# Routed attention and a feed-forward block: the second pair's rows loaded at the start, the first queries on two queues, a second PSUM bank in the last block

## The chip, the cores and the metric

The kernel runs on one core of a Trainium2 chip. The metric is the device time of one execution in microseconds (us); less is better. A core has five engines with an instruction queue each: TensorE (PE; its weight loads are shown apart as PEld), VectorE (DVE), ScalarE (ACT), GpSimd (POOL) and SyncE (SP). They wait for one another by semaphores only. Loads and stores are DMA transfers: an engine's queue issues them, here mostly SP's (queue q1 in the profile) and some ACT's (q10), and 16 DMA engines move the data.

## The reference

Routed attention over 4 batches, 8 heads, 768 tokens and head dimension 64, and then a feed-forward block over the 3072 tokens:

```python
q_assign = argmax(einsum('bhsd,hcd->bhsc', q_n, c_n))      # 16 centroids per head
k_assign = argmax(einsum('bhsd,hcd->bhsc', k_n, c_n))
mask = q_assign[:, :, :, None] == k_assign[:, :, None, :]
scores = where(mask, scale * matmul(q, k.T), -1e9)
attn = softmax(scores)
x = matmul(attn, v)                                        # -> (3072, 512)
h = x @ w_in                                               # 512 -> 2048
g = h * clip(h + 3.0, 0.0, 6.0) / 6.0
out = g @ w_out                                            # 2048 -> 512
```

A query sees only the keys whose nearest centroid is its own. All is in float32; the weights come as 64-bit floats and are decoded in the kernel.

## The kernel before, in words

Heads are worked on in pairs, two heads side by side on the 128 partitions, 16 pairs in all. The first half of the pairs (g below `FIRST` = 8) is computed with full score tiles and a mask that is added on PE; the second half is computed later from rows sorted by cluster. The feed-forward block is interleaved as filling work, and ends the kernel alone.

*What a full pair needs.* `load` (L187 to L202) brings queries and keys, 192 KB per head, into one tile `qk`, and the values into `vt`. All are issued on SP. The tile `qk` has one buffer (`qkp`), so the next pair's rows can be loaded only when this pair's are turned. `turn` (L309) turns 12 blocks of 128 x 128 on PE in three parts of four blocks. Each part goes into a PSUM tile `pqk` of the rotating pool `psum_m` (two banks), and a copy on ACT (of pair 0's third part on DVE) brings it to `xf`. `cluster_scores` multiplies with the centroids (PE tile `pcs`, L337, copied by ACT to `cs`), `route` turns that back (`pr`), takes the maximum on DVE (`mx`) and makes the `one_hot` tile; `route_turn` turns it (`po`, L379) and copies it, scaled, to `xm`, the mask operand: the first part on ACT, pair 0's second part on DVE.

*The loop.* One step treats two blocks of keys (n and n + 1, 12 blocks per pair). `scores` (L400) adds the mask product of `xm` and the product of `xf` in a PSUM tile `ps` of which there are two; `exponentials` (L423, ACT) makes `ex` from it; `key_sums` adds them up on POOL; `attn_v` (L443, PE) multiplies those of the step before with `vt` into `pv`, the single bank of `psum_v`. Between these stand, at fixed places of the order, the preparation of the next pair (`prep_items`: `turn` parts 0 and 1 in step r = 0, part 2 in r = 2, cluster scores in r = 4, and so on) and the decoding of weight chunks (`raw`, 512 KB each, three buffers; `split` runs a total on ACT, L228, and the first step on DVE, L232, into a PSUM tile of the single bank of `psum_t`). The order on every engine is the order of the Python code: nothing is rescheduled.

*The start.* The centroids are loaded on ACT's queue; queries, keys, values and a weight chunk on SP's. `idle` (L288) issues transposes of the identity whose results nobody uses: 18 before pair 0's rows, 5 between its parts, ahead of the centroids' transpose `pc` (L302), and 5 behind. Then come the cluster scores of pair 0, the unmasked part of its first scores (`scores_qk`), the routing, and the loop.

*The end.* A feed-forward block multiplies 256 tokens by a scheme with seven products (`down`, parts 0 to 6) whose results are the halves of two PSUM tiles `X` and `Y`; DVE adds (L705) and stores (`keep`, L709) give four output pieces of 128 KB. Parts 2 and 5 write the first half of `Y`, parts 3 and 6 the second. After part 6 DVE adds for two output pieces; the last is stored from ACT's queue in the last block. After it all engines branch on a flag (L1691) over a general path that is not taken.

Of the kernel before, what the change touches and what calls it, by code (L numbers as in the profile page):

```python
# [8 lines left out]
F32 = mybir.dt.float32  # L9
# [7 lines left out]
B, H, S, D = 4, 8, 768, 64  # L17
# [102 lines left out]
def fast_path(ctx, tc, ok, q, k, v, centroids, moe_w_in, moe_w_out, out):  # L120
# [60 lines left out]
    def scratch(shape, name, dtype=F32):  # L181

        if st["early"]:
            return psum_m.tile(shape, dtype, name=name, tag="m")
        return psum_t.tile(shape, dtype, name=name, tag="t")
# [3 lines left out]
    def load(g, *names):  # L189
        if g > FIRST or (g == FIRST and "v" in names):  # L190
            return
        b, h = divmod(2 * g, H)
        for name in names:
            if name == "v":
                dst = st["v", g] = vp.tile([P, 2, NCH, D], F32, name="vt")
            elif name == "q":
                st["qk", g] = qkp.tile([P, 2, NCH, 2, D], F32, name="qk")
            if name != "v":
                dst = st["qk", g][:, "qk".index(name)]
            src = {"q": q, "k": k, "v": v}[name]  # L200
            for t in range(2):
                nc.sync.dma_start((dst[:, t] if name == "v" else dst[:, :, t]), src[b, h + t].rearrange("(p j) d -> p j d", p=P))  # L202

# [64 lines left out]
    def constants():  # L270
        make_identity(nc, ident)
        for t in range(2):
            nc.vector.tensor_reduce(
                out=parity[:, t : t + 1],
                in_=ident.rearrange("p (h t c) -> p t h c", t=2, c=C)[:, t], axis=AX.XY, op=ALU.max,
            )
        nc.gpsimd.memset(half_c, 0.5)
        nc.gpsimd.memset(low_c, 1.0 / BOUND)
        nc.gpsimd.memset(ones, 1.0)
        nc.gpsimd.memset(w_low, W_LOW)  # L280
        nc.gpsimd.memset(one_hot, 0.0)

        idle(18)

    def idle(count):
        warm = psum_t.tile([P, 4, P], F32, name="warm", tag="t")
        for i in range(count):
            nc.tensor.transpose(out=warm[:, i % 4], in_=ident, identity=ident)  # L288
# [17 lines left out]

    def turn(g, part):  # L309
        if part == 0:  # L310
            st["xf", g] = xp.tile([P, NC2, P], F32, name="xf")
        qk, xf = st["qk", g], st["xf", g]
        pt = scratch([P, 4, P], "pqk")
        for i in range(4):
            j = part * 4 + i
            if g == 0 and j == NCH:

                idle(5)
                centroid_turn()
            nc.tensor.transpose(out=pt[:, i], in_=qk[:, j // NCH, j % NCH], identity=ident)  # L320
        dst = xf[:, part * 4 : part * 4 + 4]

        if g == 0 and part == 2:
            nc.vector.tensor_copy(out=dst, in_=pt)
        else:
            nc.scalar.copy(out=dst, in_=pt)
        if part == 2:
            st.pop(("qk", g))
# [63 lines left out]
    def scores_qk(n):  # L392
        st["ps", n] = psum_s.tile([P, 2, 512], F32, name="ps")
        scores_part(n, st["xf", where(n)[0]], True, False)
# [191 lines left out]
    def ffn_items(b):  # L586
# [109 lines left out]
        def product(bank, half, kind, w, first, last, again, chunks=range(HF)):  # L696
            for i in chunks:
                nc.tensor.matmul(  # L698
                    bank[:, half * HC : (half + 1) * HC], lhsT=g_sb[:, kind, i], rhs=w[:, i],
                    start=(first and i == 0), stop=(last and i == HF - 1),  # L700
                    skip_group_check=again,
                )

        def add(out_, in0, in1):
            nc.vector.tensor_tensor(out=out_, in0=in0, in1=in1, op=ALU.add)  # L705

        def down(m, part):
            def keep(chunk, half, y, queue=nc.sync):
                queue.dma_start(out_v[b, 2 * m + chunk][:, half * HC : (half + 1) * HC], y)  # L709

            def multiply(second):
                if part < 2:
                    h = range(part * HF // 2, (part + 1) * HF // 2)
                    if second:
                        product(st["X"], 1, 5, st["T2"], False, True, False, h)
                    else:
                        product(st["X"], 0, 0, wb[0][0], True, False, False, h)
                    return
                kind, bank, half, w = (
                    (4, "Y", 0, st["T1"]), (1, "Y", 1, st["T3"]),  # L720
                    (2, "X", 0, wb[1][0]), (6, "Y", 0, wb[1][1]), (3, "Y", 1, st["T4"]),
                )[part - 2]
                h = range(second * HF // 2, (second + 1) * HF // 2)
                product(st[bank], half, kind, w, part == 2, part in (3, 4, 6), part > 3, h)

            def begin():
                raise_gates()
                if part == 0:
                    pool_x = st["psum_y"] if (b, m) == (0, 0) else psum_m
                    st["X"] = pool_x.tile([P, DM], F32, name="X", tag="m")  # L730
                    st["y0"] = yp.tile([P, DM], F32, name="y0", tag="y0")
                elif part == 2:
                    pool_y = psum_m if (b, m) == (0, 0) else st["psum_y"]
                    st["Y"] = pool_y.tile([P, DM], F32, name="Y", tag="m")
                    st["y1"] = yp.tile([P, DM], F32, name="y1", tag="y1")
                multiply(0)

            def end():
                multiply(1)
                if part == 0:  # L740
                    finish()
                if (b, m, part) == (B - 1, NHC - 1, 6):
                    st["good"] = nc.values_load(ok[0:1, 0:1], min_val=0, max_val=1)
                if part == 4:
                    token_sums(*divmod(b * NHC + m + 1, NHC))
                y0, y1 = st["y0"], st.get("y1")
                if part == 1:
                    nc.scalar.copy(out=y0[:, HC:], in_=st["X"][:, HC:])
                    add(y0[:, HC:], y0[:, HC:], st["X"][:, 0:HC])
                elif part == 3:  # L750
                    add(y1[:, 0:HC], y0[:, HC:], st["Y"][:, HC:])
                    add(y1[:, HC:], y1[:, 0:HC], st["Y"][:, 0:HC])
                    keep(1, 1, y1[:, HC:])
                elif part == 4:
                    nc.scalar.copy(out=y0[:, 0:HC], in_=st["X"][:, 0:HC])
                    keep(0, 0, y0[:, 0:HC])
                elif part == 6:
                    add(y1[:, 0:HC], y0[:, HC:], st["Y"][:, HC:])
                    keep(1, 0, y1[:, 0:HC])
                    add(y0[:, HC:], y0[:, HC:], st["Y"][:, 0:HC])  # L760

                    keep(0, 1, y0[:, HC:], nc.scalar if st["last"] else nc.sync)
                if (b, m) == (0, 0):
                    for i in ([HF - 1, HF - 2], [5], [4], [], [3, 2], [0], [1])[part]:
                        make_first_sums(i)
                    if part in (0, 1):
                        weight_sums(6 + part)
                    elif part in (2, 3):
                        weight_sums(2 + part)

            return [begin, end]
# [461 lines left out]
    def prep_items(g, r):  # L1233

        if g > FIRST:
            return []
        turns = [lambda part=part: turn(g, part) for part in range(3)]
        if g == FIRST:
            return {
                0: turns[:2], 2: turns[2:], 4: [lambda: cluster_scores(g)], 6: [lambda: own_clusters(g)],  # L1240
            }.get(r, [])
        one_hots = [lambda: route_turn(g, 0), lambda: route_turn(g, 1)]
        return {
            0: turns[:2], 2: turns[2:], 4: [lambda: cluster_scores(g)], 6: [lambda: route(g)],
            8: one_hots[:1], 10: one_hots[1:],
        }.get(r, [])
# [39 lines left out]
    with tc.manual_schedule():  # L1286
        nc.scalar.dma_start(cen, centroids.rearrange("h c d -> (h c) d"))
        load(0, "q", "k")
        constants()
        load(0, "v")  # L1290
        load_weights(0)
        centroid_norm()
        for part in range(3):
            turn(0, part)
        idle(5)
        nc.vector.tensor_copy(out=ident_q, in_=ident)
        load(1, "q", "k")
        load_weights(1)
        cluster_scores(0)
        scores_qk(0)  # L1300
        route(0)
        scores_qk(1)
        for part in range(2):
            route_turn(0, part)

        for n in range(0, total + lag_d + 2, 2):
            g, r = divmod(n, per_pair)
# [418 lines left out]
```

## Time and profile before

| | |
|---|---|
| median of 3 runs | 949.89 us (947.76 to 950.37) |
| profiled execution | 947.94 us, its span 946.1 us |
| PE busy | 928.3 us, 98% of the span |
| DVE, ACT, POOL busy | 591.6, 349.5, 583.9 us |
| moved by DMA | 124.23 MB |

The span runs from the first to the last instruction of the profiled execution; the time has 1.84 us more around it. A row of the timeline has the start in us, the duration in us (of several like instructions together where "x" and a count stand at its end), engine, line, operation, output tile and inputs, and in brackets how long the engine had been idle before it and what released it. "SPq" and "ACTq" are queues that issue DMAs. A row of a table of stretches has the stretch, its length, and the busy time of each engine within it with the number of instructions.

### The profile page before, as it was taken

Reading aid. Unit: us, or ns where it says so; the run is one execution under the profiler, and the core shown is the slowest. Engines: PE = TensorE matmul, PEld = TensorE weight load, DVE = VectorE, ACT = ScalarE, POOL = GpSimd, SP = SyncE. Lnnn points to the kernel's source line nnn. Section 1 sums busy time; section 2 is a strip of 40 time slices with the busy share of each in tenths; the row PEclk is TensorE's granted clock in tenths of the full one; section 3 lists DMA queues with packets and bytes.
Section 4 is the critical chain, followed back from the end, with each engine's and each line's share of the span. In section 5 each row is a group of like instructions: output and inputs, shape, how many; then the busy total and the mean of one; then the engine's idle time right before and its main releaser. Section 6 shows DMA issues by size and latency. Waiting matters only on the chain.

```text
span 946.1 us, 17635 instructions
## 1 busy us (share of the span) xinstructions
PE 928.3 (98%) x6358; PEld 726.5 (77%) x6358; DVE 591.6 (63%) x1294; ACT 349.5 (37%) x731; POOL 583.9 (62%) x1314
## 2 busy tenths in 40 slices
PE   8999999989999999999999999999999999999997
PEld 5444444555798798797887988978888799999996
DVE  6789889899976375284483474564571554536261
ACT  5888877766112232233232132241331311212020
POOL 3878777769366677787777777777777060303030
PEclk9999999999999999999999999999999999999999
DMA  7345555361364648482683654754753233323120
GB/s 192 108 134 157 134 156 165 109 174 46 96 209 141 153 137 175 130 220 78 171 201 100 166 158 128 192 151 113 176 161 99 77 99 113 106 69 110 56 68 26
DMA packets 174351, 124.23 MB, mean 131 GB/s; under 512 B 134064, under 2 KB 152496, under 8 KB 174256
## 3 DMA queue, kind: packets, MB, share of 16 engines
q1 hardware_dynamic: 151936, 76.04, 31.2%
q10 hardware_dynamic: 13104, 34.38, 12.7%
q0 software_dynamic: 9216, 12.60, 4.4%
q8 instruction: 52, 0.85, 0.4%
q14 instruction: 43, 0.35, 0.1%
HBM read 94.67 MB, written 28.31 MB: 130 GB/s over the span
## 4 chain that ended last, share of the span: by engine, by line
PE 70%; DVE 2%; DMA 1%; ACT 0%; POOL 0%; issue 0%; SPq 0%; ACTq 0%
PE Y L698 18%; PE uY L659 15%; PE X L698 13%; PE uX L659 12%; PE pv L1116 3%; PE ps L1077 3%; PE ps L919 2%; PE pv L1077 1%; PE pd L1140 1%; PE pcs L337 1%; PE ps L1157 1%; DMA piece<-kvd 1%; DVE g_sb L649 0%; DVE g_sb L502 0%; DVE g_sb L670 0%; DVE sx L670 0%
## 5 line engine op out<-in xcount | busy, mean ns | idle before, releaser
L433 POOL TENSOR_TENSOR acc<-acc,ex 128x768 f32<-128x768 f32 x64 | 123.8, 1935 | 26.0 <-ACT ex L423 22.4
L1034 POOL DMA_INDIRECT qd<-qn,pos x96 | 96.3, 1003 | 44.9 <-issue 32.5
L1050 POOL DMA_INDIRECT xn<-xsd,pos x96 | 93.7, 976 | 48.8 <-DVE g_sb L649 27.1
L499 ACT ACTIVATE sx<-g_sb,half_c 128x512 f32<-128x512 f32 x88 | 63.7, 724 | 141.1 <-DVE g_sb L670 141.1
L649 POOL TENSOR_TENSOR g_sb<-g_sb 128x256 f32<-128x256 f32 x52 | 39.1, 773 | 123.6 <-DVE g_sb L502 122.6
L1034 POOL DMA_INDIRECT kvd<-kvn,pos x96 | 96.6, 1006 | 25.6 <-issue 25.6
L1026 POOL MEMSET w_low<- 128x1 f32 x864 | 90.9, 105 | 33.3
L705 DVE TENSOR_TENSOR y<-y,Y 128x256 f32<-128x256 f32 x48 | 20.2, 421 | 136.5 <-PE Y L698 135.7
L659 PE MATMUL uX<-xb,w_in_sb 128*128 128x128 f32 x704 | 93.0, 275 | 0.0
L698 PE MATMUL X<-w_out_sb,g_sb 128*128 128x256 f32 x384 | 90.6, 382 | 0.4 <-DVE g_sb L502 0.4
L698 PE MATMUL Y<-T,g_sb 128*128 128x256 f32 x384 | 88.0, 381 | 0.0
L698 PE MATMUL Y<-w_out_sb,g_sb 128*128 128x256 f32 x384 | 87.7, 380 | 0.0
L659 PEld LDWEIGHTS uX<-xb,w_in_sb 128*128 128x128 f32 x704 | 85.7, 192 | 0.0
L698 PEld LDWEIGHTS X<-w_out_sb,g_sb 128*128 128x128 f32 x384 | 70.9, 190 | 14.8 <-issue 3.9
L698 PEld LDWEIGHTS Y<-T,g_sb 128*128 128x128 f32 x384 | 72.1, 190 | 13.2 <-issue 3.9
L670 DVE TENSOR_TENSOR sx<-uX,sx 128x128 f32<-128x128 f32 x176 | 51.0, 290 | 49.3 <-ACT sx L677 45.7
L698 PEld LDWEIGHTS Y<-w_out_sb,g_sb 128*128 128x128 f32 x384 | 71.9, 190 | 10.6 <-issue 1.3
L400 PE MATMUL ps<-xf 64*128 64x384 f32 x384 | 78.6, 487 | 0.3 <-ACT ex L423 0.3
L423 ACT ACTIVATE ex<-ps 128x768 f32<-128x768 f32 x96 | 72.6, 802 | 4.6 <-PE ps L400 4.5
L443 PE MATMUL pv<-ex,vt 128*64 128x384 f32 x384 | 72.5, 499 | 0.0
L502 DVE SCALAR_TENSOR_TENSOR g_sb<-sx,g_sb 128x512 f32<-128x512 f32 x88 | 63.6, 725 | 3.4 <-ACT sx L499 3.4
L670 DVE TENSOR_TENSOR g_sb<-uY,sx 128x128 f32<-128x128 f32 (+1 forms) x176 | 65.5, 413 | 0.0
(196 smaller groups left out, 1805.5 us busy)
## 6 DMA issues: line engine op xcount, KB each, us to landing
tx<-td ACTq DMA_DIRECT2D x86, 384.0 KB, 3.5
raw<-in_moe_w_in_dram SPq DMA_DIRECT2D x16, 512.0 KB, 3.8
raw<-in_moe_w_out_dram SPq DMA_DIRECT2D x16, 512.0 KB, 3.2
xb<-xd SPq DMA_DIRECT2D x12, 512.0 KB, 4.3
out_dram<-y SPq DMA_DIRECT2D x44, 128.0 KB, 1.7
qk<-in_q_dram SPq DMA_DIRECT2D x18, 192.0 KB, 3.7
qk<-in_k_dram SPq DMA_DIRECT2D x18, 192.0 KB, 5.0
vt<-in_v_dram SPq DMA_DIRECT2D x16, 192.0 KB, 3.8
```

The costliest lines, as they stand in the source:

```text
L400: nc.tensor.matmul(st["ps", n][:, t, 0:HALF], lhsT=x[r, NCH + j], rhs=x[r, hf * NHC : (hf + 1) * NHC], start=first, stop=last, skip_group_ ...
L423: nc.scalar.activation(out=ex, in_=sc, func=ACT.Exp, scale=SM_SCALE)
L433: nc.gpsimd.tensor_tensor(out=acc, in0=acc, in1=ex, op=ALU.add)
L443: nc.tensor.matmul(pv[t * D : (t + 1) * D], lhsT=vt[:, t, j], rhs=ex[:, t], start=(j == 0), stop=(j == NCH - 1),)
L499: nc.scalar.activation(out=r, in_=h, func=ACT.Relu, bias=half_c, scale=1.0 / 6.0)
L502: nc.vector.scalar_tensor_tensor(out=g, in0=r, scalar=1.0, in1=h, op0=ALU.min, op1=ALU.mult)
L659: nc.tensor.matmul(dst, lhsT=w[:, kt], rhs=x(kt), start=(kt == 0), stop=(kt == HK - 1))
L670: nc.vector.tensor_tensor(out=out_, in0=in0, in1=in1, op=ALU.add)
L698: nc.tensor.matmul(bank[:, half * HC : (half + 1) * HC], lhsT=g_sb[:, kind, i], rhs=w[:, i], start=(first and i == 0), stop=(last and i == ...
L1026: nc.gpsimd.memset(w_low, W_LOW)
L1034: i = nc.gpsimd.indirect_dma_start(out=rows[name, g, t], in_=src, in_offset=None, out_offset=bass.IndirectOffsetOnAxis(ap=pos[:, a, j, t : ...
L1050: nc.gpsimd.indirect_dma_start(out=xn[:, j, t], out_offset=None, in_=rows["xsd", g, t], in_offset=bass.IndirectOffsetOnAxis(ap=pos[:, 0, j ...
```

## The change

Four things are changed; the lines of this diff have the parts that are spoken of.

- Pair 1's queries and keys get room of their own: a part of `g_sb`, the tile of the feed-forward block, which is written by that block only later. So their load is issued directly behind pair 0's, ahead of the first values and weight chunks.
- Pair 1's three `turn` parts leave the loop. They stand in the start: the first between `scores_qk(1)` and the transposes of the one-hot tile, the two others behind these. Parts 0 and 2 use the bank of `psum_v`, part 1 that of `psum_t`.
- The second of pair 0's two query transfers is issued on ACT's queue, behind the centroids. The idle transposes are 16, none and 4, where they were 18, 5 and 5.
- In the last block `Y`'s second half has a tile of its own, `Y1`, so the first half is complete after part 5; its sum is taken there, written to a spare tile `z` and stored from SP's queue. Behind part 6 one sum and one store are left.

```diff
             elif name == "q":
-                st["qk", g] = qkp.tile([P, 2, NCH, 2, D], F32, name="qk")
+                if g == 1:
+                    spare = g_sb.rearrange("p k i c -> p (k i c)")[:, 0 : NC2 * P]
+                    st["qk", g] = spare.rearrange("p (a j t d) -> p a j t d", a=2, j=NCH, t=2)
+                else:
+                    st["qk", g] = qkp.tile([P, 2, NCH, 2, D], F32, name="qk")
...
-                nc.sync.dma_start(...)
+                queue = nc.scalar if (g, name, t) == (0, "q", 1) else nc.sync
+                queue.dma_start(...)
...
-        idle(18)
+        idle(16)
...
-    def turn(g, part):
+    def turn(g, part, bank=None):
...
-        pt = scratch([P, 4, P], "pqk")
+        pt = bank if bank is not None else scratch([P, 4, P], "pqk")
...
-                idle(5)
                 centroid_turn()
...
+            closing = (b, m) == (B - 1, NHC - 1)
...
-                    (4, "Y", 0, st["T1"]), (1, "Y", 1, st["T3"]),
-                    (2, "X", 0, wb[1][0]), (6, "Y", 0, wb[1][1]), (3, "Y", 1, st["T4"]),
+                    (4, "Y", 0, st["T1"]), (1, "Y1", 1, st["T3"]),
+                    (2, "X", 0, wb[1][0]), (6, "Y", 0, wb[1][1]), (3, "Y1", 1, st["T4"]),
...
+                    st["Y1"] = pool_y.tile([P, DM], F32, name="Y", tag="m") if closing else st["Y"]
...
+                elif part == 5 and closing:
+                    z = sxp.tile([P, 4, P], F32, name="sx").rearrange("p k c -> p (k c)")[:, 0:HC]
+                    add(z, y0[:, HC:], st["Y"][:, 0:HC])
+                    keep(0, 1, z)
                 elif part == 6:
-                    add(y1[:, 0:HC], y0[:, HC:], st["Y"][:, HC:])
+                    add(y1[:, 0:HC], y0[:, HC:], st["Y1"][:, HC:])
                     keep(1, 0, y1[:, 0:HC])
-                    add(y0[:, HC:], y0[:, HC:], st["Y"][:, 0:HC])
-                    keep(0, 1, y0[:, HC:], nc.scalar if st["last"] else nc.sync)
+                    if not closing:
+                        add(y0[:, HC:], y0[:, HC:], st["Y"][:, 0:HC])
+                        keep(0, 1, y0[:, HC:], nc.scalar if st["last"] else nc.sync)
...
+        if g == 1:
+            turns = []
...
         load(0, "q", "k")
+        load(1, "q", "k")
         constants()
...
-        idle(5)
+        idle(4)
         nc.vector.tensor_copy(out=ident_q, in_=ident)
-        load(1, "q", "k")
         load_weights(1)
         cluster_scores(0)
         scores_qk(0)
         route(0)
         scores_qk(1)
+        def values_bank():
+            return psum_v.tile([P, 512], F32, name="pv").rearrange("p (i c) -> p i c", i=4)
+        turn(1, 0, values_bank())
         for part in range(2):
             route_turn(0, part)
+        turn(1, 1, psum_t.tile([P, 4, P], F32, name="pqk", tag="t"))
+        turn(1, 2, values_bank())
```

More of the change, by code (lines that the diff above doesn't have):

```diff
@@ L201, in load @@
             for t in range(2):
-                nc.sync.dma_start((dst[:, t] if name == "v" else dst[:, :, t]), src[b, h + t].rearrange("(p j) d -> p j d", p=P))
+                queue = nc.scalar if (g, name, t) == (0, "q", 1) else nc.sync
+                queue.dma_start((dst[:, t] if name == "v" else dst[:, :, t]), src[b, h + t].rearrange("(p j) d -> p j d", p=P))
     chunks = weight_chunks(w_in_sb, w_out_sb, moe_w_in, moe_w_out)
@@ L719, in multiply @@
                 kind, bank, half, w = (
-                    (4, "Y", 0, st["T1"]), (1, "Y", 1, st["T3"]),
-                    (2, "X", 0, wb[1][0]), (6, "Y", 0, wb[1][1]), (3, "Y", 1, st["T4"]),
+                    (4, "Y", 0, st["T1"]), (1, "Y1", 1, st["T3"]),
+                    (2, "X", 0, wb[1][0]), (6, "Y", 0, wb[1][1]), (3, "Y1", 1, st["T4"]),
                 )[part - 2]
                 h = range(second * HF // 2, (second + 1) * HF // 2)
-                product(st[bank], half, kind, w, part == 2, part in (3, 4, 6), part > 3, h)
+                product(st[bank], half, kind, w, part == 2 or closing and part == 3, part in ((2, 3, 4, 5, 6) if closing else (3, 4, 6)), part > 3, h)
             def begin():
@@ L756, in end @@
                     keep(0, 0, y0[:, 0:HC])
+                elif part == 5 and closing:
+                    z = sxp.tile([P, 4, P], F32, name="sx").rearrange("p k c -> p (k c)")[:, 0:HC]
+                    add(z, y0[:, HC:], st["Y"][:, 0:HC])
+                    keep(0, 1, z)
                 elif part == 6:
-                    add(y1[:, 0:HC], y0[:, HC:], st["Y"][:, HC:])
+                    add(y1[:, 0:HC], y0[:, HC:], st["Y1"][:, HC:])
                     keep(1, 0, y1[:, 0:HC])
-                    add(y0[:, HC:], y0[:, HC:], st["Y"][:, 0:HC])
-                    keep(0, 1, y0[:, HC:], nc.scalar if st["last"] else nc.sync)
+                    if not closing:
+                        add(y0[:, HC:], y0[:, HC:], st["Y"][:, 0:HC])
+                        keep(0, 1, y0[:, HC:], nc.scalar if st["last"] else nc.sync)
                 if (b, m) == (0, 0):
```

## The prediction

> **What bounds the kernel now.** I read the page of the profile first, then a table of stretches, then the start, the first loop steps and the tail in order of time.
>
> ```profile
> span 946.1 us, 17635 instructions
> ...
> PE 928.3 (98%) x6358; PEld 726.5 (77%) x6358; DVE 591.6 (63%) x1294; ACT 349.5 (37%) x731; POOL 583.9 (62%) x1314
> ...
> PE 70%; DVE 2%; DMA 1%; ACT 0%; POOL 0%; issue 0%; SPq 0%; ACTq 0%
> ```
> ```profile
> 5.15:9.61 4.46, 4.07 (x25) 3.58 (x24) 1.50 (x5) 1.17 (x2) 0.00 (x0) 1.00 0.76 234
> ...
> 14.79:44.00 29.21, 29.13 (x199) 13.46 (x199) 23.35 (x27) 25.81 (x56) 21.77 (x12) 1.00 0.48 140
> ...
> 182.00:250.00 68.00, 64.78 (x380) 37.30 (x379) 65.85 (x73) 41.16 (x90) 52.64 (x41) 1.00 0.38 111
> ```
>
> The first three lines: PE is busy for 928.3 of 946.1 us and carries the chain that ended last. The columns of the stretches are length, then busy time of PE, PEld, DVE, ACT and POOL, granted clock, DMA share and GB/s. From 14.79 on PE has hardly a gap (29.13 of 29.21 us), ACT a small reserve (25.81). Later, in 182 to 250, DVE is full as well (65.85 of 68). So only two kinds of gain count: the loop begins sooner, or PE has less to do in it. Behind the first two loop steps the order of instructions on every engine is the same in both kernels until the tail, so a shift won at 23 us should be carried to the end.
>
> **The start.** The rows in order of time (start, duration, what):
>
> ```profile
> 0.74 1.35 SPq L202 DMA_DIRECT2D qk<-in_q_dram  x2
> ...
> 1.36 3.70 PEld L288 LDWEIGHTS warm<-ident 128*128 128x128 f32 x18 [1.36 <-POOL ident masks.py:199]
> ...
> 2.14 1.34 SPq L202 DMA_DIRECT2D qk<-in_k_dram  x2
> ...
> 5.15 1.20 PEld L320 LDWEIGHTS pqk<-ident,qk 128*128 128x128 f32 x6
> ...
> 6.33 1.08 PEld L288 LDWEIGHTS warm<-ident 128*128 128x128 f32 x5
> 6.35 0.59 ACT L326 COPY xf<-pqk 128x512 f32<-128x512 f32 x1 [1.52 <-PE pqk L320]
> ...
> 7.75 0.14 PEld L302 LDWEIGHTS pc<-ident,cenwide 128*128 128x128 f32 x1 [0.34 <-PE warm L288]
> ...
> 7.82 0.68 PEld L320 LDWEIGHTS pqk<-ident,qk 128*128 128x128 f32 x6
> ...
> 8.47 0.58 PEld L288 LDWEIGHTS warm<-ident 128*128 128x128 f32 x5
> ...
> 8.78 0.69 DVE L324 COPY xf<-pqk 128x512 f32<-128x512 f32 x1 [0.36 <-PE pqk L320]
> ...
> 9.61 0.85 PE L337 MATMUL pcs<-xf,cnT 128*32 128x384 f32 x8 [0.33 <-DVE ident_q L1296]
> ```
> ```profile
> DMA to landing us min/median/max: 3.4/3.4/3.4
> ```
> ```profile
> q1 hardware_dynamic: 3206, 0.89, 69.2%
> ```
>
> The first loose line is the landing of the first query transfer, 3.4 us behind its issue; the second says that queue q1 had moved 0.89 MB by 6.1 us, so nearly all of the first pair's four loads (4 x 192 KB = 0.79 MB) had come by then.
>
> *First queries on two queues.* One transfer leaves SP (1.35 / 2 = 0.67 us of issue) for ACT, where it stands behind the centroids' load. The queries were needed at 5.15, where the 18 idle transposes had just run out (1.36 + 3.70 = 5.06). With 16 of them that is 1.36 + 16 x 0.206 = 4.65. The second query transfer was issued at 0.74 + 0.67 = 1.41 and, with the same 3.4 us, in at about 4.8; from ACT it is issued some 0.3 us sooner, but then shares the engines with the first keys. I take the first transposes to start at 5.0 (between 4.65 and 5.2). What is delayed on ACT by 0.67 us is a table load for the centroids' norm; the norm's result is first needed by the transpose "pc", behind the query transposes, so it costs nothing, and at most these 0.67 us if that cover went.
>
> *The five idle transposes between.* They kept PE from 6.33 to 7.41, and "pc" and the key transposes stood behind them. Without them "pc" follows the queries' transposes at about 6.3, and the next bound is late instead: the keys, whose last load was issued at 2.14 + 0.67 = 2.81, in at 6.2 by the 3.4 us, and 0.67 sooner issued now; I take 6.5. The last four transposes also wait for the first copy out of their bank (6.35 + 0.59 = 6.94, now about 6.8). They run at 0.20 us each until the clock steps up (1.20 / 6 = 0.20, then 1.08 / 5 = 0.22, but 0.68 / 6 = 0.11 from 7.82 on; the clock column shows 1.00 all along, so the durations decide), hence end at about 7.65 where they ended at 8.50. DVE's copy moves from 8.78 to about 8.0, and "pcs" from 9.61 to 8.8: **-0.8 us**. Bounds: -1.5 (keys at 6.2, all six at 0.11) and +0.5 (the clock rival below). Nothing is lost by four instead of five idle ones at 8.47, which lie beside DVE's copy.
>
> *Pair 1 (the second) ahead on SP.* Four issues of 0.67 us stand before the first values and weights. By 6.1 us what is left before the first weight chunk is complete is 0.79 (pair 1) + 0.39 (values) + 0.52 (weights) - 0.10 = 1.6 MB; at the 234 GB/s of the stretch 5.15 to 9.61 that is 6.8 us, so 12.9, a little more with the landing. Pair 1's queries are in at 8.5 or so, its keys by 10.2. The users:
>
> ```profile
> 11.72 0.92 PE L400 MATMUL ps<-xf 64*128 64x384 f32 x4
> ...
> 12.91 0.84 PE L379 MATMUL po<-ident_q,one_hot 128*128 128x128 bf16 x12 [0.28 <-DVE one_hot L357]
> 13.46 0.81 ACT L384 ACTIVATE xm<-po 128x768 bf16<-128x768 bf16 x1 [2.46 <-PE po L379]
> 13.79 0.56 DVE L382 TENSOR_SCALAR xm<-po 128x768 bf16<-128x768 bf16 x1 [0.67 <-PE po L379]
> 14.27 0.68 DVE L232 TENSOR_SCALAR wtop<-raw 128x512 uint32<-128x512 uint32 x1
> ...
> 14.41 0.50 PE L400 MATMUL ps<-xm 64*128 64x384 bf16 x4 [0.65 <-DVE xm L382]
> 14.79 1.51 ACT L423 ACTIVATE ex<-ps 128x768 f32<-128x768 f32 x2 [0.52 <-PE ps L400]
> ...
> 14.84 1.09 PE L320 MATMUL pqk<-ident,qk 128*128 128x128 f32 x8
> ...
> 15.86 0.34 PE L400 MATMUL ps<-xm 64*128 64x384 bf16 x2
> ...
> 16.18 1.08 ACT L326 COPY xf<-pqk 128x512 f32<-128x512 f32 x2
> ...
> 17.12 0.70 ACT L228 ACTIVATE wsize<-raw 128x512 bf16<-128x512 f32 x1
> ...
> 17.58 1.51 PE L443 MATMUL pv<-ex,vt 128*64 128x384 f32 x8
> ...
> 18.67 1.49 ACT L423 ACTIVATE ex<-ps 128x768 f32<-128x768 f32 x2
> ...
> 19.02 0.66 PE L320 MATMUL pqk<-ident,qk 128*128 128x128 f32 x4
> ...
> 19.61 0.34 PE L400 MATMUL ps<-xm 64*128 64x384 bf16 x2
> ```
>
> Values are used at 17.58, weights at 14.27 on DVE: hidden. If weights came a microsecond late, DVE would lose it, which had 29.21 - 23.35 = 5.9 us idle in that stretch.
>
> **Twelve transposes moved.** PE saves 1.09 + 0.66 = 1.75 us in the loop. But the eight at 14.84 stood in the wait for the first exponential to free its bank (the next scores at 15.86), so they were nearly free; and the scores at 19.61 needed the exponentials of 18.67, which were late on ACT, not on PE. So ACT's own chain is the measure. Before: mask copy at 13.46, a wait of 0.52, two exponentials 1.51, two copies 1.08, two weight totals (17.12 to 18.67 = 1.55), next exponentials at 18.67. After: the copy of the first four (about 0.59) runs ahead of the mask copy where ACT was idle for 2.46, but its four transposes end near 13.0, so it pushes the mask copy from 13.46 to 13.6; the two others now stand before the first exponential. 13.6 + 0.81 + 1.08 + 1.51 + 1.55 = 18.55 instead of 18.67: **-0.1 us**, with the first exponential later (15.5 instead of 14.79) and the third copy gone behind it. DVE's first weight step shares the bank of the second four and waits for their copy, some 0.7 us, into its idle time. Bounds: -1.75 if PE's saving all counted, +0.6 if one copy (0.59) were added to ACT's chain whole.
>
> **The tail.**
>
> ```profile
> 930.70 10.35 SPq L709 DMA_DIRECT2D out_dram<-y  x3
> ...
> 940.27 0.87 DVE L705 TENSOR_TENSOR y<-y,Y 128x256 f32<-128x256 f32 x2 [9.23 <-PE Y L698]
> 941.17 0.34 ACTq L709 DMA_DIRECT2D out_dram<-y  x1
> ```
> ```profile
> L1691 SPq EVENT_SEMAPHORE  x8: 17/17/17, 943.9 to 944.4; - x8
> ...
> L1691 SPq COMPARE_BRANCH  x1: 45/45/45, 941.1 to 941.1; - x1
> ```
> ```profile
> SPq L1691 <- SPq L1691: 2.8, 1, 2.8
> ```
>
> With a bank of its own one of the two last sums runs four microseconds sooner, and the store on ACT goes (941.17 + 0.34 = 941.51). The other sum and its store on SP stay where they were, ending at 930.70 + 10.35 = 941.05. And SP then shows the longest row of the end: a branch at 941.1 and nothing until 943.9, 2.8 us, whatever ACT does. Only if ACT's store is what the end waits for is the gain 941.51 - 941.05 = 0.46. Bounds -0.46 and 0; I take **-0.1**, nearer to SP's row.
>
> **Sum.** -0.8 - 0.1 - 0.1 = -1.0 us. The profiled execution took 947.94 us (span 946.1 and 1.84 around it), so 946.9 for its like. It lies 1.95 below the median of 949.89; the forecast for the median is 949.89 - 1.0 = **948.9 us**.
>
> **Rivals.** *The clock steps up later (slower).* PE ran its transposes slowly from 1.36 until after 7.41, six microseconds of nearly unbroken work. Now it pauses between 4.65 and about 5.0 and again before the keys. If the step slips behind "pcs" and the first scores, these run at half speed: 0.85 more for "pcs", some 0.3 of the 0.92 of the scores that ACT's copy doesn't cover, 0.15 in the transposes: 1.3 us. The sum becomes +0.3, 950.2; from a slip of about a microsecond and a half it decides the sign. The Trainium skill, "TensorE: Matmul & The Clock Gate", section "Part 1: The HAM clock gate (the "warmup" mystery)", has a free-running window of about 3.4 us that must be busy before full clock is granted; by it a pause in the wrong window costs a whole further window, and the slow rows here agree with a step after one to two windows. Chance 0.2, mostly within 0.3%.
>
> *The queues bring nothing.* Both queues feed the same transfer engines, and the first queries may land at 5.0 as before, the keys at 6.7. Then the first copy ends at 6.94 as before and the sum loses 0.1 to 0.2: 949.1. This is the case of "DMA: Bandwidth & Descriptors", section "Issuing engines are not separate DMA queues" of the Trainium skill: a second issuing engine saves only the issue time; no row of before has two queues loading at once. Chance 0.2, the same verdict as mine.
>
> *Everything counts (faster).* Start -1.1, PE's saving whole (-1.75, ACT catching up by its reserve), tail -0.46: -3.3, 946.6. Against it stands ACT's chain above. Chance 0.25.
>
> **Numbers.** Forecast 0.3, queues 0.2, clock 0.2, everything 0.25, and 0.05 for something unseen that costs more, such as a later load held up. Faster by over 0.3% (under 947.0; about what a measurement of this kernel can tell from no change) 0.25; slower by over 0.3% (above 952.7) 0.08: the unseen, and the clock slipping twice; within it 0.67. The range takes the fast rival and a microsecond of spread (the runs before lie between 947.76 and 950.37): 945.6; and the clock rival with as much: 951.3.
>
> **What would show it.** Right: key transposes start before 7, "pcs" near 8.8, the first exponentials begin later against "pcs" than before, the scores at 19.61 come near 18.7; the last sum on DVE alone at PE's end and SP's 2.8 us unchanged behind it. Wrong: slow transposes beyond 8.5; a load named as releaser of PE at the first "pv"; an end that moves up by half a microsecond against PE's last matmul.

## The result and the profile after

The changed kernel takes 948.54 us (median of 18 executions, 946.34 to 951.47), the kernel before 950.38 beside it (18 executions, 947.76 to 952.41). The ratio is 0.9981 with a 95% interval of 0.9972 to 0.9990: 1.8 us less, between 0.95 and 2.7. The forecast was 948.9.

The profiled executions go the other way: 948.64 us after (span 946.8) against 947.94 before (span 946.1). So the two traces must not be subtracted end from end; they are followed from the start. The page of the changed kernel:

```profile
span 946.8 us, 17619 instructions
...
PE 927.3 (98%) x6350; PEld 724.9 (77%) x6350; DVE 589.2 (62%) x1294; ACT 349.6 (37%) x731; POOL 586.6 (62%) x1314
...
PE 64%; POOL 5%; DMA 2%; issue 2%; DVE 1%; SPq 0%; ACT 0%; POOLq 0%; ACTq 0%
```

PE is still what bounds it. It is busy for 1.0 us less than before, and yet the span is 0.7 longer. The start of the changed kernel, in order of time:

```profile
1.16 0.62 ACTq L207 DMA_DIRECT2D qk<-in_q_dram  x1
...
5.06 0.84 PE L324 MATMUL pqk<-ident,qk 128*128 128x128 f32 x6 [0.29 <-DMA qk<-in_q_dram]
5.66 0.14 PEld L307 LDWEIGHTS pc<-ident,cenwide 128*128 128x128 f32 x1
...
6.83 0.64 PEld L324 LDWEIGHTS pqk<-ident,qk 128*128 128x128 f32 x6 [1.04 <-issue]
6.86 0.84 PE L324 MATMUL pqk<-ident,qk 128*128 128x128 f32 x6 [0.85 <-DMA qk<-in_k_dram]
...
8.58 0.85 PE L341 MATMUL pcs<-xf,cnT 128*32 128x384 f32 x8 [0.44 <-DVE ident_q L1310]
...
14.36 1.56 ACT L427 ACTIVATE ex<-ps 128x768 f32<-128x768 f32 x2
...
18.43 0.34 PE L404 MATMUL ps<-xm 64*128 64x384 bf16 x2
```

"pc" follows the query transposes at once. The key transposes then wait 0.85 us for the keys' landing, and six of them take 0.64 us, 0.11 each: here the clock was up when they began. "pcs" starts at 8.58 instead of 9.61, the third pair of masked scores at 18.43 instead of 19.61, so the changed kernel enters its loop 1.18 us ahead. This lead is kept for 170 us, and then gone at one place. The exponentials of ACT on both sides of it, first of the kernel before, then of the changed one:

```profile
188.90 1.49 ACT L423 ACTIVATE ex<-ps 128x768 f32<-128x768 f32 x2
...
207.65 1.49 ACT L423 ACTIVATE ex<-ps 128x768 f32<-128x768 f32 x2
```
```profile
187.73 1.49 ACT L427 ACTIVATE ex<-ps 128x768 f32<-128x768 f32 x2
...
208.10 1.49 ACT L427 ACTIVATE ex<-ps 128x768 f32<-128x768 f32 x2
```

1.17 us ahead at 188, 0.45 behind at 208: 1.62 us lost. Between them lies a pause of PE that both kernels have, ahead of the masks of a later pair; first before, then after:

```profile
196.25 0.51 PE L379 MATMUL po<-ident_q,one_hot 128*128 128x128 bf16 x6 [2.26 <-DVE one_hot L357]
```
```profile
195.07 0.51 PE L383 MATMUL po<-ident_q,one_hot 128*128 128x128 bf16 x6 [2.25 <-DVE one_hot L361]
```

The pause is the same, but not what follows it. The stretches below are 3.41 us long and set so that their borders fall on the changes of the granted clock in each trace (columns: length, busy time of PE, PEld, DVE, ACT, POOL, then the granted clock); first before, then after:

```profile
191.76:195.18 3.42, 2.23 (x14) 0.77 (x12) 3.28 (x6) 1.11 (x2) 3.26 (x3) 1.00 0.39 87
195.18:198.59 3.41, 2.34 (x20) 1.34 (x22) 3.31 (x7) 1.76 (x4) 1.28 (x1) 1.00 1.12 286
```
```profile
192.09:195.51 3.42, 1.17 (x12) 0.40 (x8) 3.32 (x7) 0.00 (x0) 3.11 (x2) 1.00 0.75 221
195.51:198.92 3.41, 3.41 (x16) 1.53 (x16) 3.34 (x4) 3.24 (x10) 0.00 (x0) 0.50 1.20 244
```

Before, the pause lay across a border: PE was busy for 2.2 and 2.3 us of two stretches, and the clock stayed at 1.00. After, the whole pause lay within one stretch, PE was busy for 1.17 of 3.42 us, and the next stretch ran at 0.50: it did half of its work, 1.7 us' worth, and the jump is 1.62. This turns the changed kernel's lead into a lag, and has nothing to do with the lines that were changed. At PE's last matmul the lag is 0.80 us; where the other 0.35 came from was not followed.

The end of the changed kernel, its last sums, its last store on SP, and the branches of the last line:

```profile
937.61 0.42 DVE L709 TENSOR_TENSOR sx<-y,Y 128x256 f32<-128x256 f32 x1 [5.78 <-PE Y L702]
941.06 0.42 DVE L709 TENSOR_TENSOR y<-y,Y 128x256 f32<-128x256 f32 x1 [3.03 <-PE Y L702]
```
```profile
941.51 0.33 SPq L715 DMA_DIRECT2D out_dram<-y  x1
```
```profile
L1711 SPq EVENT_SEMAPHORE  x8: 17/17/17, 944.6 to 945.1; - x8
...
L1711 SPq COMPARE_BRANCH  x1: 45/45/45, 941.9 to 941.9; - x1
```

One sum stands alone behind PE's end, and the store on ACT is gone. SP's branch still takes from 941.9 to 944.6, 2.7 us.

### The profile page after: what moved, and what is told of

It is laid out like the page before. It is cut to its first block, busy times and chain, and to the rows that moved or that the text cites. A ratio compares the mean times of both kernels' runs of the same rounds, so it can differ in the third digit from the quotient of the medians.

```text
span 946.8 us, 17619 instructions
## 1 busy us (share of the span) xinstructions
PE 927.3 (98%) x6350; PEld 724.9 (77%) x6350; DVE 589.2 (62%) x1294; ACT 349.6 (37%) x731; POOL 586.6 (62%) x1314
## 4 chain that ended last, share of the span: by engine, by line
PE 64%; POOL 5%; DMA 2%; issue 2%; DVE 1%; SPq 0%; ACT 0%; POOLq 0%; ACTq 0%
PE Y L702 16%; PE uY L663 14%; PE X L702 12%; PE uX L663 11%; PE pv L1127 3%; PE ps L1088 2%; PE ps L930 2%; POOL qd L1045 1%; POOL xn L1061 1%; POOL w_low L1037 1%; PE pv L1088 1%; POOL kvd L1045 1%; DMA tx<-td 1%; PE pd L1151 1%; DMA vs<-kvd 0%
## 5 line engine op out<-in xcount | busy, mean ns | idle before, releaser
L1045 POOL DMA_INDIRECT qd<-qn,pos x96 | 98.2, 1023 | 44.6 <-issue 32.7
```

Source lines behind the costliest of these rows:

```text
L1045: i = nc.gpsimd.indirect_dma_start(out=rows[name, g, t], in_=src, in_offset=None, out_offset=bass.IndirectOffsetOnAxis(ap=pos[:, a, j, t : ...
```

## The experiments

The theory at this point: the start is worth what "pcs" moves, the moved transposes 0.16 us, queues and tail nothing; and a pause of PE of 2 us costs 1.6 us more in those executions in which it falls into one clock window. The rivals: the queues or the tail carry a part; or the clock is a by-product and only the pauses' length counts.

The runs named after_again, e6, e9 and e10 were on a chip on which the kernel before takes 957.83 us; the others on one where it takes 950.1 to 950.9. Ratios are always to the kernel before on the same chip, as they stand on record; they are not quite the quotients of the two medians (946.89 by 950.14 in the second run of e4 would be 0.9966, and the record has 0.9954).

**The idle transposes alone** (e1): the kernel before with only these edits.

```diff
-        idle(18)
+        idle(16)
-                idle(5)
                 centroid_turn()
-        idle(5)
+        idle(4)
```

> The kernel before with only the idle transposes changed (16, none, 4). My theory: the five idle transposes ahead of pc were what held the start, so pcs starts at 8.6 to 8.9 instead of 9.61 when the clock steps up late, and is bounded by the keys' landing (about 6.8); from pcs to the third pair of masked scores it stays 10.0 us as before (9.61 to 19.61). Time 0.5 to 1.0 us under before. Rival (the moved transposes bring the gain): pcs moves by under 0.3 us or the loop gives it back, time within 0.3 us of before. Rival (the clock steps up a window later because PE pauses): pcs at or behind 9.6, time 0.3 or more over before.

Measured: 949.29 us, ratio 0.9982 (0.9970 to 0.9994). "pcs" starts at 8.78, and the third masked scores 10.00 us behind it, as before. This part alone has the size of the whole change.

**Rows and moved transposes alone** (e2): the changed kernel with its idle transposes, first queue and tail undone.

```diff
-        idle(16)
+        idle(18)
+                idle(5)
                 centroid_turn()
-        idle(4)
+        idle(5)
-                queue = nc.scalar if (g, name, t) == (0, "q", 1) else nc.sync
+                queue = nc.sync
-            closing = (b, m) == (B - 1, NHC - 1)
+            closing = False
```

> The kernel before with only the second pair's rows loaded early and turned in the routing; idle transposes 18, 5, 5, one queue, tail as before. My theory: pcs within 0.1 of 9.6 for a late clock step, from pcs to the third pair of masked scores 9.85 instead of 10.0 us, because ACT's chain and not PE decides; time 0.15 us under before, not to be told from it. Rival (PE's saved 1.75 us count): 8.3 to 9.0 from pcs to the third pair, time 1.0 to 1.75 us under before.

Measured: 950.19 us, ratio 0.9992 (0.9980 to 1.0004). The third masked scores come 9.84 us behind "pcs". This distance was 10.00 in each of the four profiles without the moved transposes (before, e1, e10, e12) and 9.84 or 9.85 in the nine with them (e6, below, apart): the transposes are worth 0.16 us, whenever the clock stepped up. "pcs" started at 8.98 here, although all of the idle transposes were back. What differed from the kernel before was when the clock stepped up: at 6.16 us instead of 7.44 (where the trace's records of the granted clock begin; the durations change there).

**One queue** (e8): the changed kernel with all first loads on SP.

```diff
-                queue = nc.scalar if (g, name, t) == (0, "q", 1) else nc.sync
+                queue = nc.sync
```

> The changed kernel with all of the first loads on SP's queue. By the rival of the prediction that the queues bring nothing: the first query transposes start at 5.0 to 5.3 either way, the keys' transposes at 6.8 to 7.1, the product with the centroids at 8.6 to 8.9, and the median is within 0.4 of the changed kernel. If the second queue carries the start's gain: the product at 9.3 or later and 0.6 us slower.

Its start:

```profile
5.01 1.51 PE L324 MATMUL pqk<-ident,qk 128*128 128x128 f32 x6
...
7.06 0.85 PE L324 MATMUL pqk<-ident,qk 128*128 128x128 f32 x6 [0.43 <-DMA qk<-in_k_dram]
...
8.79 0.85 PE L341 MATMUL pcs<-xf,cnT 128*32 128x384 f32 x8 [0.44 <-DVE ident_q L1310]
```

Measured: 946.99 us, ratio 0.9961 (0.9944 to 0.9977). The query transposes start at 5.01 on one queue and at 5.06 on two, and "pcs" at 8.79 lies among the starts with two queues (8.58 to 9.04). So the second queue brings nothing. Two queues may even cost something: the median of the six executions is 1.5 us under the changed kernel's, and the intervals of the two ratios overlap only from 0.9972 to 0.9977. No row of the start shows a reason, and it was not followed further.

**The old tail** (e7):

```diff
-            closing = (b, m) == (B - 1, NHC - 1)
+            closing = False
```

> The changed kernel with the old tail: one bank for the last block's second result, its last two sums together at PE's end, and a store on ACT's queue behind them. By the prediction the end is SP's branch of 2.7 us and the store on ACT hardly counts: from PE's last matmul to the end 0.0 to 0.4 longer than with the new tail, the median within 0.5. If ACT's store set the end: 0.5 or more on every execution.

```profile
941.52 0.87 DVE L709 TENSOR_TENSOR y<-y,Y 128x256 f32<-128x256 f32 x2 [9.23 <-PE Y L702]
```
```profile
L1711 SPq EVENT_SEMAPHORE  x8: 17/17/17, 945.1 to 945.6; - x8
...
L1711 SPq COMPARE_BRANCH  x1: 45/45/45, 942.3 to 942.3; - x1
```

Measured: 948.70 us, ratio 0.9980 (0.9967 to 0.9993), the changed kernel's own. From PE's last matmul to the end it takes 5.87 us here and 5.82 in the changed kernel. SP's branch starts 0.8 to 0.9 us behind PE's end and takes 2.7 to 2.8 us in both. Without the slower chip the tail takes 5.87 to 6.48 in its old form (before, e1, e2, e7, e12) and 5.71 to 6.13 in its new one (after, e3, e4 twice, e8): 0.3 us lie between the means, and they are not told apart from its own spread.

**No idle transposes first** (e6): the changed kernel without the first sixteen, to see what a late clock costs.

```diff
-        idle(16)
```

> The changed kernel without the first 16 idle transposes: PE starts cold with the first query transposes at 5.0 us. This gives the price of a late clock step. By the rival of the prediction the step slips behind the product with the centroids and the first scores: PE's clock steps up at 8.5 to 12 us, the product starts at 8.8 to 9.3 instead of 8.58, and the median is 0.5 to 1.5 above the changed kernel, 949 to 950. If the step does not matter (keys bound the start and ACT's chain covers the rest): within 0.3 of the changed kernel.

```profile
5.51 1.51 PE L323 MATMUL pqk<-ident,qk 128*128 128x128 f32 x6 [5.51 <-DMA qk<-in_q_dram]
...
7.32 1.51 PE L323 MATMUL pqk<-ident,qk 128*128 128x128 f32 x6
...
9.70 1.34 PE L340 MATMUL pcs<-xf,cnT 128*32 128x384 f32 x8
...
20.03 0.34 PE L403 MATMUL ps<-xm 64*128 64x384 bf16 x2
```

The clock stepped up at 10.74, in the middle of "pcs" (1.34 us instead of 0.85), which started at 9.70, later than expected. The third masked scores came at 20.03. In the control beside it (after_again, clock up at 7.32) they came at 18.70, 1.33 us sooner; but 0.34 of this is the landing of the first queries, whose transposes started at 5.51 here and at 5.17 there. In e3 they started at 5.51 too, with the clock up at 4.93, and the scores came at 18.89. So the late clock costs some 1.0 to 1.1 us. The whole time, 959.16 from four executions with a ratio of 0.9999 (0.9964 to 1.0034), is too wide to show it. The control:

> The changed kernel once more, as a control beside the next three. Both theories: a median of 948 to 949, and executions spread over 946 to 951 as before. By the clock theory (a pause of PE of 2 us that falls into one clock window costs a half-speed window of 3.41 us, some 1.6 us) the slow executions are those with a lower mean granted clock, some 0.7 us for each 0.001. By the rival (spread of the transfers) mean clock and time have nothing to do with each other.

It took 954.85 us, ratio 0.9973 (0.9945 to 1.0001), with "pcs" at 8.86.

**PE kept busy in the first pause** (e3): 18 extra transposes into unused columns.

```diff
-        pd = scratch([P, 512], "pd")
-        pd = pd[:, 0:HALF]
+        whole_pd = scratch([P, 512], "pd")
+        pd = whole_pd[:, 0:HALF]
...
+        if n == 77:
+            for _ in range(18):
+                nc.tensor.transpose(out=whole_pd[:, HALF : HALF + P], in_=ident, identity=ident)
```

> The changed kernel with 18 idle transposes on PE in its longest pause of the attention part (2.25 us behind pd, at 192.8). My theory: that pause costs the full clock for one window of 3.41 us (1.6 us of time) whenever it falls within one window, which depends on the execution and happened in the profiled one of the changed kernel; with the pause filled no half clock is granted between 20 and 300 us, and the mean is 0.3 to 0.8 us under the changed kernel's, so about 2.2 to 2.6 us under before. Rival (the drop has another cause): a half clock window still appears in that part, time as the changed kernel's 1.8 us under before. Rival (the idle transposes get in the way): po starts later than 2.25 us behind pd, time over the changed kernel's.

```profile
193.26 2.18 PE L477 MATMUL pd<-ident 128*128 128x128 f32 x18
195.58 0.51 PE L383 MATMUL po<-ident_q,one_hot 128*128 128x128 bf16 x6
```

Measured: 948.51 us, ratio 0.9977 (0.9963 to 0.9991), hardly another time than the changed kernel's. The pause near 194 is filled, and no half-speed window followed it; but in the profiled execution one came at 486.21 to 489.62, behind a second pause of PE (for the reload of the W1 differences, `tx<-td`). One execution says nothing on how often; the time alone doesn't show that the filling helps.

**Both pauses filled** (e9 the changed kernel, e10 the kernel before): as e3, and this in the W1 step 37.

```diff
                 part(Y[:, 3], wi(1, 1, i), s(2))
+                if u == 37:
+                    for _ in range(19):
+                        nc.tensor.transpose(out=X[:, 3], in_=ident, identity=ident)
```

> The changed kernel, with 18 extra transposes of the identity issued into PE's pause ahead of the masks near 193 us and 19 into the one ahead of the W1 product near 484 us. The waits stay as long, PE is only kept busy in them. Clock theory: no half-speed window between 20 us and PE's last matmul, and a median of 947.2 (946.6 to 947.8), 1.3 under the changed kernel, with half its spread. Rival theory (the pauses' own length counts, the clock is a by-product): 948.5 and no narrower; if the extra transposes delay work, up to 949.

> The kernel before with the same extra transposes in the same two pauses. Clock theory: 948.2 (947.7 to 949), some 2 under the kernel before, and 1.0 to 1.2 over the changed kernel treated alike, which is the change's own worth: the start (1.0) and the transposes (0.1). Rival: the whole 1.8 between the two kernels is the change's, and stays between the filled ones too.

Measured: 960.97 us (ratio 1.0035, 1.0011 to 1.0058) and 962.55 (1.0054, 1.0029 to 1.0078): slower, where faster was expected. The second filling went wrong, as PE's waits of e9 show (who waits, for whom, us in total, times, longest):

```profile
PE uX L697 <- DVE sx L678: 4.3, 1, 4.3
PE uX L667 <- DVE sx L678: 2.3, 1, 2.3
```

The extra transposes write a bank that DVE still reads, so they stood 4.3 us in the queue themselves and made the pause longer. A second wait of 2.3 us (2.1 in e10) came up near 283, which only these two kernels have; how it hangs on the edit wasn't found. Neither time tells anything on the clock, and the 1.6 us between the two are not told apart from the 1.0 to 1.2 or the 1.8 that were expected. But the start of e10, far ahead of the edit, is the kernel before once more, with another moment of the clock's step (4.44 us):

```profile
5.94 0.58 PEld L288 LDWEIGHTS warm<-ident 128*128 128x128 f32 x5
...
7.00 0.64 PEld L320 LDWEIGHTS pqk<-ident,qk 128*128 128x128 f32 x6
...
8.75 0.85 PE L337 MATMUL pcs<-xf,cnT 128*32 128x384 f32 x8 [0.33 <-DVE ident_q L1303]
```

The five idle transposes are there, at 0.12 us each, and yet the key transposes start at 7.00, as in the kernels without them (6.83 to 7.29), and "pcs" at 8.75, as early as in the changed kernel.

**A shorter pause** (e4): the masks near 194 us wait for DVE, which is decoding weights; two decoding steps are moved from the loop step 76 to 78.

```diff
     def share(n, r):
+        if n in (76, 78):
+            return {76: 2, 78: 5}[n]
```

> The changed kernel with two weight decoding steps of DVE (0.69 and 0.70 us) put behind the seventh pair's routing sums instead of ahead of them. My theory: PE's pause before po shrinks from 2.25 to about 0.85 us, everything behind it comes 1.4 us earlier, and no window is idle enough to lose the clock: 1.4 to 2.0 us under the changed kernel, 3.2 to 3.8 under before. Rival (DVE is full between 182 and 250, so the two steps are only paid at the next wait for it): the pause shrinks, but the first feed-forward work moves by under 0.5 us.

> The changed kernel with two decoding steps moved from the loop step 76 to 78, once more. If the shorter pause of PE ahead of the masks (0.78 instead of 2.25 us) is worth its length (1.5) and the half-speed window that it sometimes brings (1.6, in some 4 of 10 executions): 2.1 under the changed kernel, so 0.9960 of the kernel before. If the first measurement (0.9951) was luck: 0.998.

The same edit in the kernel before (e12):

> The kernel before with the same two decoding steps moved, without the change. The pause near 194 us is the same in both kernels, so the same gain of 2.1 is expected: 0.998 of the kernel before, and 0.002 over the changed kernel with the two steps moved, which is the change's own worth in a pair without that pause (1.2 us by the start's shift). Rival: the change and the moved steps touch the same time, and this kernel comes within 0.5 us of the other.

The first masks behind the pause in e4 and in e12:

```profile
193.92 0.51 PE L383 MATMUL po<-ident_q,one_hot 128*128 128x128 bf16 x6 [0.78 <-DVE one_hot L361]
```
```profile
194.81 0.51 PE L379 MATMUL po<-ident_q,one_hot 128*128 128x128 bf16 x6 [0.80 <-DVE one_hot L357]
```

Measured: e4 945.87 us, ratio 0.9951 (0.9934 to 0.9968), and once more 946.89, ratio 0.9954 (0.9937 to 0.9971): the first measurement was not luck. e12 946.99, ratio 0.9967 (0.9953 to 0.9980). In e12 the masks come 1.44 us sooner than in the kernel before, from a start that is the same within 0.02 us ("pcs" at 9.63 and 9.61). The three profiles have no half-speed window before PE's last matmul. In the kernel before this edit brings 3.1 us, more than the 2.1 expected; what the rest is stays open. By the medians it is worth more than the whole change (1.8), though the intervals of the two ratios overlap (0.9953 to 0.9980, 0.9972 to 0.9990), and with the change it beats both kernels (946.3 is the median of e4's twelve executions). Between e12 and these twelve lie 0.7 us, the change's worth without that pause. That the two touch the same time isn't excluded by it: of the two medians of e4 one lies 1.1 us under e12, the other 0.1.

## Why the prediction was right, and where its steps were not

The time (948.5 for a forecast of 948.9) and the verdict within 0.3% came as said. That the two times are so close is in part luck: the forecast took 1.0 us off a kernel before of 949.89, the median of three executions, and measured were 1.8 us off 950.38; 1.0 lies just inside the interval (0.95 to 2.7). The terms did less well than the sum.

**The start, -0.8.** In the profiled pair "pcs" moved by 1.03, and the next bound was the keys' landing, as said, though later (6.86 for 6.5); the key transposes ran at 0.11 instead of 0.20 us, and the two differences nearly cancel. But the term was read off one execution, in which the clock stepped up only at 7.44, and taken as the kernel's own. With the idle transposes in place "pcs" starts at 8.75, 8.98, 9.61 and 9.63 for a clock that steps up at 4.44, 6.16, 7.44 and 7.47 (e10, e2, before, e12; mean 9.24). Without them it starts at 8.58 to 9.04 in nine profiles with steps from 4.36 to 7.32, in no order (mean 8.82; one of the four and two of the nine on the slower chip): there the keys decide, and "pcs" follows the key transposes by 1.72 or 1.73 us in eight of the nine. So the edit gains from nothing to 1.0 us, some 0.4 over these few profiles. This is the step that was mis-sized: the slow rows were put down to the kernel, and they belonged to the phase of the clock. The profile of before could have told: its own durations (0.20, 0.22, then 0.11 us) change in the middle of equal work.

**The transposes, -0.1.** The size is right (0.16), the chain only in part. ACT holds PE up, as said, but at the first exponentials: they start 5.78 us behind "pcs" where it was 5.18, and PE waits 1.09 us for the first of them. From there PE works without a gap up to the scores at 18.43, so these do not wait for the second exponentials, by which the prediction measured them:

```profile
15.26 0.34 PE L404 MATMUL ps<-xm 64*128 64x384 bf16 x2 [1.09 <-ACT ex L427]
...
16.98 1.51 PE L447 MATMUL pv<-ex,vt 128*64 128x384 f32 x8
...
17.31 1.49 ACT L427 ACTIVATE ex<-ps 128x768 f32<-128x768 f32 x2
```

The second exponentials moved by 0.33 us against "pcs" (8.73 behind it, where it was 9.06), not by 0.12. The sum of 18.55 adds up durations that overlap in the trace: the same sum from the rows of before gives 18.93, where the exponentials started at 18.67. So that the term came out as said is in part luck.

**The tail, -0.1.** Right within its spread: SP's branch of 2.7 us stands last in both forms, and taking the store off ACT's queue brings nothing that can be told from the spread.

**The rivals.** "The queues bring nothing" is true of the queues (e8), but not of the start, whose gain came from the idle transposes; it was priced as if both fell together. By "DMA: Bandwidth & Descriptors", section "Issuing engines are not separate DMA queues" of the Trainium skill, a second issuing engine saves only the time of issuing; the query transposes at 5.01 on one queue and 5.06 on two agree. (That no row of before has two queues loading at once, as the prediction says, overlooks the centroids, issued on ACT at 0.74 together with the first queries on SP.) "The clock steps up later" didn't happen in any profile of the changed kernel with its sixteen idle transposes; its price of 1.3 us was about right (e6: 1.0 to 1.1). The clock came in at another place: a pause in the wrong window, 190 us later and in both kernels. "Everything counts" fell: PE's wait for ACT's first exponentials held its saving at 0.16.

**What stays open.** Some 0.4 us at the start, 0.16 from the transposes and up to 0.3 from the tail make 0.6 to 0.9, and the measured gain is 1.8 with an interval that begins at 0.95. The idle transposes alone (e1) measured 1.6 us where four starts against nine give 0.4. Whether executions of the kernel before draw a late clock, or a half-speed window, more often than the few profiles show can't be said from one profiled execution per kernel. That of before is a lucky draw: it has no half-speed window and lies 2.4 us under its median.

The record has more on this, the mean granted clock of every execution. In the 51 executions of the kernel before beside e1 to e4, e7, e8 and e12 the time goes with it: the median is 951.45 us in the 31 at 0.996 or less, and 949.04 in the 14 at 0.998 or more, some 0.7 us for each 0.001. This is what was expected of after_again, whose own six executions don't show it (the four at 0.999 took 952.5 to 959.6). The median clock is 0.996 in these 51 and 0.998 in the changed kernel's eighteen. But it also counts the time behind PE's last matmul, when PE has no work left, and there the profile of before has 0.71 and the changed one 0.97; e7, with the old tail, has a median of 0.997 at the changed kernel's time. One half-speed window lowers the mean clock by 0.0018, which makes 1.3 us by this slope and 1.62 by the traces. So the clocks agree roughly with the price of such a window, and leave open whether the missing microsecond lies in them.

## What to carry to other kernels

Before a gain is summed from one profiled execution, ask which of its durations belong to the kernel and which to the clock's phase in that execution; an equal instruction that changes its duration in the middle is the sign. Follow two traces by the lead of one engine over the other from the start, and look for the jump, instead of comparing their ends. And look for the longest pauses of the bounding engine in the rest of the kernel: shortening one of 2.25 us by moving two steps of DVE's decoding brought 3.1 us in the kernel before, and the whole change 1.8.

## What the runs showed of the hardware

A pause of PE that is shorter than a clock window can halve its clock. In the fourteen profiles there are eight stretches at 0.50 before PE's last matmul. Each is 3.41 us long, or one window, and starts a whole number of windows behind the first step up. In the window ahead of each PE was busy for 0 to 1.28 of 3.41 us, and every window with so little work was followed by one; no window with 1.41 us (41%) or more was. Both pauses of e7 show it in one execution:

```profile
193.38:196.79 3.41, 1.54 (x16) 1.08 (x18) 3.31 (x7) 1.00 (x2) 2.00 (x2) 1.00 0.98 275
196.79:200.21 3.42, 3.42 (x20) 1.79 (x17) 3.33 (x3) 3.36 (x10) 0.44 (x1) 1.00 1.24 267
483.51:486.93 3.42, 1.07 (x9) 1.10 (x10) 3.25 (x11) 0.87 (x2) 2.68 (x9) 1.00 1.11 290
486.93:490.34 3.41, 3.41 (x23) 3.29 (x22) 2.74 (x11) 1.57 (x3) 2.88 (x9) 0.50 0.72 178
```

1.54 us of work in a window (45%) and the next runs at 1.00; 1.07 us (31%) and the next runs at 0.50. The Trainium skill, "TensorE: Matmul & The Clock Gate", section "Part 1: The HAM clock gate (the "warmup" mystery)", has the free-running window of 3.4 us, and the traces agree (3.41). The section of the Trainium skill on oscillation ("HAM oscillation — how this bites in real kernels", same page) warns of pauses of more than a window; here 2.25 us was enough where it fell within one, and cost 1.62 us on top of itself. Since the phase is another in each execution, such a pause makes the time of one kernel spread, and a profile shows one draw of it. That the half-speed windows follow from the pauses rests on these fourteen profiles; no run set the phase.
